# One more step of a weight conversion in five items of an attention head, and half the zero products in its last items

## The chip, the cores and the metric

The kernel runs on one core of one Trainium2 chip. The metric is the device time of one execution in microseconds (us). Its engines are named as in the profile: PE (TensorE, its weight loads as PEld), DVE (VectorE), ACT (ScalarE), POOL (GpSimd) and SP (SyncE, which here only issues DMAs).

## The reference, cut to what matters

```python
def reference(q, k, v, s, x..., w_in, w_out, domain_probs, w1, w2):
    # attention: 2 batches x 8 heads, 576 positions, 64 wide
    cum = np.cumsum(np.maximum(s, 0.0), axis=-1)
    bias = -(cum[:, :, :, None] - cum[:, :, None, :])
    scores = np.where(causal, -1e9, scale * q @ k.T + np.minimum(bias, 0.0))
    attn = softmax(scores)
    x = (attn @ v) with the heads side by side      # 1152 x 512
    # a layer of 512 -> 2048 -> 512
    h = x @ w_in
    x = np.maximum(0.01 * h, h) @ w_out
    # four experts of 512 -> 1024 -> 512
    p = domain_probs / (domain_probs.sum(-1, keepdims=True) + 1e-09)
    out += p[:, e:e + 1] * (np.maximum(x @ w1[e], 0.0) @ w2[e])     # for e in 0 to 3
```

All of it is fp32 in the reference. The kernel receives `w_in` and `w_out` as 64-bit numbers and turns them into the bits of fp32 values on the chip: that is the weight conversion that the change is about.

## The kernel before, in words

All work is in one function, `attention_moe_moe2`, and every instruction of an engine is recorded through one helper, so that all have the line L43 in the profile and are told apart by the names of their tiles. In the first phase, up to about 220 us, the order on each engine is the order in which the program is written (`fixed`), so an instruction waits for all that was written ahead of it on its engine. A product in fp32 quality is made from split operands: a value is cast to a rounded type (ACT, `CAST`) and the rest is what a subtraction leaves (DVE or POOL, `TENSOR_TENSOR`).

The first phase has three strands that are woven by hand.

- **Attention**, the generator `attention()` (`side`). It works in items; an item is one tile of 128 queries of one head. Its steps for an item are the scores (PE, `ps_sc`, then a custom instruction on DVE that adds the mask and takes the minimum, `z`), the exponential (ACT, `z<-z,mn`), the transposes (PE, `ps_pt`, copied by ACT to `pv`), the values (PE, `ps_o`) and, behind a pair of heads, the scaling (DVE `st`, `xo`) and the transposed result (PE `ps_x`, ACT and DVE `x`). Items overlap: while the scores of item i are made, the transposes are those of item i-3. The generator yields three times an item. The scores have two PSUM buffers, the transposes two, the values one.
- **The weight conversion**, the generator `supply()`. It has 16 units of 128 x 1024 numbers (512 KB of fp32). A unit's raw 64-bit numbers are fetched to a tile `r` (1024 KB, two buffers). Then come ACT `raw<-r` (absolute value and scale), two DVE `TENSOR_SCALAR` (limits, shift), two DVE `SCALAR_TENSOR_TENSOR raw<-r,raw` (bits, sign). A unit's finished fp32 numbers are stored to DRAM (`w_f<-raw`) and the unit after next is fetched. In the head of the phase (`heading`) the unit is also split on the spot, by an ACT `CAST w<-raw` of 128 x 1024 and a DVE `TENSOR_TENSOR w<-raw,w`, and store and fetch are issued on ACT's queue. Units converted behind the head store and fetch on POOL's queue, and their split is made by `late_splits()`: SP loads 512 KB back (`raw<-w_f`), and ACT and DVE split it in halves of 128 x 512. One call of `next(units_of_w)` makes one step: seven steps a unit in the head, six behind it.
- **The layer**, the generator `main`, whose products are `ps_u` and `ps_d` on PE, with `ht` on ACT and DVE.

The head is the loop `for at_ in range(3*64)` over attention's yields; it ends in item 39. In it `CONVERTING` lists the items below 31 whose third yield takes a step of the conversion; from item 31 on each takes one. At the first two yields of each item from 31 on, `onto_held()` lets PE multiply a tile of zeros (128 x 128, two records each: `ps_u<-idle`) onto a bank that is held for a sum; it changes no value. Behind the head the loop `for at_, i in enumerate(side)` weaves the three strands, and the loop over `main` behind it brings the rest of the layer, late splits and, on DVE and POOL, sums and products for the second half (`sums`, `t`, `w<-sums`).

Of the kernel before, what the change touches and what calls it, by code (L numbers as in the profile page):

```python
# [19 lines left out]
def attention_moe_moe2(ctx: ExitStack, tc: tile.TileContext, q, k, v, s, w_in, w_out, probs, w1, w2, out):  # L20
# [107 lines left out]
    def late_splits():  # L128

        nonlocal reading  # L130
        while len(ready) < CONVERTED:
            n = len(ready)
            if n < min(retired + WB + 2, stored):
                reading, raw = True, kept.pop(n, None)
                if raw is None:
                    raw = load_w(*stream[n][:3])
                    for _ in range(5):
                        yield
                while n >= retired + WB:
                    yield  # L140

                w = wpool.tile([P, 2, 1024], F32R, tag="w", name="w")
                for part in (slice(0, 512), slice(512, 1024)):
                    nc.scalar.copy(w[:, 0, part], raw[:, part])
                    (nc.gpsimd if n == CONVERTED - 1 else nc.vector).tensor_tensor(w[:, 1, part], raw[:, part], f32(w[:, 0, part]), ALU.subtract)
                ready.append(w.rearrange("p l (a b) -> p l a b", a=stream[n][1][0]))
                reading = False
            else:
                yield
# [564 lines left out]
    def idling(n):  # L714

        for _ in range(n):
            nc.tensor.matmul(nothing[:, :P], idle[:, :P], idle[:, :P], start=True, stop=True)
# [3 lines left out]
    def onto_held():  # L721

        nc.tensor.matmul(held[2][:, :P], idle[:, :P], idle[:, :P], start=False, stop=False, skip_group_check=True)
# [19 lines left out]
    def pads(pool):  # L743

        for i in range(3):
            x, y = (pool.tile([P, 2, half[0]], F32, name=f"{of}e{i}") for of in "qk")
            q_e.append(x)
            k_e.append(y)
        for i in range(3):
            nc.gpsimd.memset(k_e[i][D:], 0.0)  # L750
            nc.gpsimd.memset(q_e[i][D:], 0.0)
            nc.gpsimd.memset(q_e[i][D:DK], 1.0)
            if i == 0:
                nc.gpsimd.memset(mask, 0.0)
                nc.gpsimd.affine_select(mask[:, S - P :], mask[:, S - P :], [[-1, P]], ALU.is_ge, MASKED, 0, 1)
            for x in v_s[i : 4 if i == 2 else i + 1]:
                nc.gpsimd.memset(x[:, :, 0 :: 2 * D + 1], 1.0)
                nc.gpsimd.memset(x[: P - S % P, QT - 1], 0.0)
        ones = pool.tile([P, 2, QC], F32, name="ones")
        nc.gpsimd.memset(ones[D:DK], 1.0)  # L760
        for x in q_s:
            nc.gpsimd.memset(f32(x[:, :, 0, QC:]), 0.0)
        own = mask2[:, P - LAST :]
        nc.gpsimd.memset(mask2, 0.0)
        nc.gpsimd.affine_select(own, own, [[-1, LAST]], ALU.is_ge, MASKED, -D, 1)
        nc.gpsimd.memset(own[:D], 0.0)
        nc.gpsimd.affine_select(own[:D], own[:D], [[-1, LAST]], ALU.is_ge, MASKED, 0, 1)
        return ones
# [236 lines left out]
    def attention():  # L1005

        nonlocal ending
        items, starts, n = [], {}, 0
        i, split = 0, iter(())
        while n < units or i < len(items) + 8:  # L1010
            if n < units and i == len(items):
                u = Unit(n)
                starts[n] = i
                items += [(u, *of) for of in u.items]
                if n + 2 < units and not 0 <= n + 2 - 2 * NP < 2:
                    load_keys(n + 2)
                    if n + 2 < 2 * NP:
                        decay(n + 2, k_e[(n + 2) % 3])
                if n in (2 * NP - 3, 2 * NP - 2):
                    load_keys(n + 3)  # L1020
                n += 1
            if n < units - 1 and i == starts[n - 1] + 2:
                load_values(n + 1)
            if i == starts[n - 1] and 2 * NP <= n < units:
                split = split_keys(n)
            for step, lag in STEPS:
                if 0 <= i - lag < len(items):
                    u, *of = items[i - lag]
                    step(u, *of)
                if lag == 1:  # L1030
                    next(split, None)
                if lag == 0 and i in CAST_AT:
                    cast_keys(2 * NP + CAST_AT.index(i), lowest[0])
                if lag in (1, 3, 7):

                    late = i - 5 + (lag == 7)
                    ending = lag != 3 and 0 <= late < len(items) and items[late][1:] == items[late][0].items[-1]
                    yield i
            i += 1

    def hidden_pool(stack, n):
        nonlocal hpool
        hpool = stack.enter_context(tc.tile_pool(name="hpool", bufs=n))
# [6 lines left out]
    with ExitStack() as phase:  # L1050
        x_t[0] = phase.enter_context(tc.tile_pool(name="x0pool", bufs=1)).tile([P, 2, KD, sizes[0]], F32R, name="x0")
        wpool = phase.enter_context(tc.tile_pool(name="wpool", bufs=4))
        r64p = phase.enter_context(tc.tile_pool(name="r64p", bufs=2))

        OPENED = (24, 25, 26, 27, 28, 29, 31, 33, 35)

        CONVERTING = (*range(5, 16), *range(17, 31, 2))
        side, units_of_w, late, opened = attention(), supply(), late_splits(), 0
        nothing = ps_mm.tile([P, 512], F32, tag="mm", name="nothing")
        with tc.tile_pool(name="early", bufs=1) as early:  # L1060
            ones = pads(early)
            sums = cumulative()
            next(sums)
            main = mlps(phases[0])

            for at_ in range(3 * 64):
                i = next(side)
                if done == 2 * NP and at_ % 3 == 2:
                    break
                if at_ % 3 == 0 and i in (6, 8):  # L1070
                    nc.scalar.copy(q_s[i // 2 - 3][D:DK, 1, :, :QC], ones[D:DK])
                if at_ % 3 == 1:
                    if i < 18:
                        idling(2 if i < 6 else 1)
                    elif opened < len(OPENED) and i >= OPENED[opened] and opened < 3 * (done // 2):
                        next(main)
                        opened += 1
                if at_ % 3 < 2 and i >= 31:
                    onto_held()
                if at_ % 3 == 2:  # L1080
                    if i == 3:
                        fetch64(1)
                    if i in (3, 4, 5):
                        next(sums)
                    if i in CONVERTING or i >= 31:
                        next(units_of_w)
        hidden_pool(phase, 6)
        heading = False

        owed = 0  # L1090
        for at_, i in enumerate(side):
            if at_ % 3 < 2:
                owed += WOVEN * KD / (2.0 * (40 - 6))
                while owed >= 1.0:
                    next(main)
                    owed -= 1.0
            if at_ % 3 != 1:
                next(late, None)
            if (at_ % 3 != 1 or i % 3 == 0) and not ending:
                next(units_of_w, None)  # L1100
        attn.close()
        w7pool = ctx.enter_context(tc.tile_pool(name="w7pool", bufs=2, side="right"))
        sumpool = phase.enter_context(tc.tile_pool(name="sumpool", bufs=2))
        scratch = phase.enter_context(tc.tile_pool(name="scratch", bufs=2))
        t7pool = ctx.enter_context(tc.tile_pool(name="t7pool", bufs=1, side="right"))
        tokens = paired_steps(1, x_t[1], t7pool)
        banks.close()
        ps_mm = Eight(ps_mm, ctx.enter_context(tc.tile_pool(name="ps_more", bufs=5, space=PSUM)))

        sevens = first_sevens()  # L1110
        for m, _ in enumerate(main):
            if m % 2 == 0:
                next(late, None)
            if (m % 3 == 0 or m == 19) and m not in (12, 15):
                next(tokens, None)
            if m % 4 == 2:
                next(units_of_w, None)
            if m % 4 % 2 and m >= 4:
                next(sevens, None)
        for _ in sevens:  # L1120
            pass
        for _ in tokens:
            pass
# [72 lines left out]
```

## Time and profile before

| | us |
|---|---|
| median of three runs | 698.78 |
| the three runs | 698.61, 701.58, 698.78 |
| the profiled execution | 699.07 |
| its span, first to last instruction | 697.3 |
| busy in the span: PE, DVE, ACT, POOL | 677.7, 475.8, 352.5, 406.0 |

Times of rows are microseconds from the start of the span. A timeline row has the start, the busy time of the row's instructions, the engine, the line, the operation with its output and inputs, how many instructions are in the row, and in brackets how long the engine was idle ahead of it and what ended that. Starts of neighbouring instructions overlap a little, since an engine begins one before the other has left. The clock in the windows is the granted share of TensorE's full clock.

### The profile page before, as it was taken

Reading aid. Unit: us, or ns where it says so; the run is one execution under the profiler, and the core shown is the slowest. Engines: PE = TensorE matmul, PEld = TensorE weight load, DVE = VectorE, ACT = ScalarE, POOL = GpSimd, SP = SyncE. Lnnn points to the kernel's source line nnn. Section 1 sums busy time; section 2 is a strip of 40 time slices with the busy share of each in tenths; the row PEclk is TensorE's granted clock in tenths of the full one; section 3 lists DMA queues with packets and bytes.
Section 4 is the critical chain, followed back from the end, with each engine's and each line's share of the span. In section 5 each row is a group of like instructions: output and inputs, shape, how many; then the busy total and the mean of one; then the engine's idle time right before and its main releaser. Section 6 shows DMA issues by size and latency. Waiting matters only on the chain.

```text
span 697.3 us, 12008 instructions
## 1 busy us (share of the span) xinstructions
PE 677.7 (97%) x4496; PEld 623.7 (89%) x4496; DVE 475.8 (68%) x1040; ACT 352.5 (51%) x727; POOL 406.0 (58%) x386
## 2 busy tenths in 40 slices
PE   8899999899998999999999999999999999999998
PEld 7778778778787999999999989999899899998997
DVE  6878899998697458837855747647657376465564
ACT  5768978876544566533634525325244253261520
POOL 5100212221198887861997949949679498495830
PEclk9999999999999999999999999999999999999999
DMA  7798689746631321101011110111202111112003
GB/s 217 197 244 205 198 224 276 218 154 211 241 122 62 121 91 62 62 1 61 1 61 62 61 61 30 63 31 61 61 1 62 61 34 58 32 62 61 1 16 120
DMA packets 43050, 69.15 MB, mean 99 GB/s; under 512 B 6432, under 2 KB 26672, under 8 KB 42992
## 3 DMA queue, kind: packets, MB, share of 16 engines
q1 hardware_dynamic: 33744, 40.30, 19.9%
q0 software_dynamic: 6016, 20.71, 9.6%
q10 hardware_dynamic: 3232, 7.38, 3.3%
q8 instruction: 35, 0.57, 0.4%
q14 instruction: 23, 0.19, 0.1%
HBM read 57.54 MB, written 10.82 MB: 98 GB/s over the span
## 4 chain that ended last, share of the span: by engine, by line
PE 71%; DVE 8%; issue 8%; DMA 7%; ACT 3%; POOL 2%; SPq 0%; ACTq 0%; POOLq 0%; DVEq 0%
PE ps_d L43 35%; PE ps_u L43 33%; DMA r<-in_moe_w_out_dram 3%; DVE t L43 2%; DMA qr<-in_q_dram 2%; DMA r<-in_moe_w_in_dram 1%; PE ps_sc L43 1%; DVE sums L43 1%; DVE raw L43 1%; PE ps_o L43 1%; DVE z L43 1%; PE ps_pt L43 1%; DMA ke<-cum 1%; ACT raw L43 1%; DVE y L43 1%
## 5 line engine op out<-in xcount | busy, mean ns | idle before, releaser
L43 PE MATMUL ps_u<-t,w 128*128 128x320 f32 (+1 forms) x1680 | 237.7, 301 | 4.1 <-DVE t L43 2.9
L43 POOL TENSOR_TENSOR w<-raw,w 128x512 fp32r<-128x512 f32 (+2 forms) x118 | 185.9, 1595 | 94.2 <-ACT w L43 93.9
L43 PEld LDWEIGHTS ps_u<-t,w 128*128 128x128 f32 x1680 | 231.4, 191 | 5.5 <-DVE t L43 3.2
L43 PE MATMUL ps_d<-w,ht 128*128 128x256 f32 (+1 forms) x1164 | 195.4, 326 | 0.1
L43 PEld LDWEIGHTS ps_d<-w,ht 128*128 128x128 f32 x1164 | 173.3, 190 | 18.6 <-PE ps_u L43 0.4
L43 ACT CAST w<-raw 128x512 fp32r<-128x512 f32 (+2 forms) x138 | 98.2, 740 | 127.0 <-PE ps_d L43 69.7
L43 ACT ACTIVATE ht<-ps_u 128x320 fp32r<-128x320 f32 (+2 forms) x160 | 68.6, 439 | 99.2 <-DVE ps_u L43 71.1
L43 PE MATMUL ps_d<-ht,w 128*128 128x320 f32 (+1 forms) x576 | 109.1, 340 | 0.2 <-DVE ht L43 0.2
L43 PEld LDWEIGHTS ps_d<-ht,w 128*128 128x128 f32 x576 | 91.4, 188 | 6.6 <-DVE ht L43 0.6
L43 POOL TENSOR_TENSOR raw<-raw 128x256 f32<-128x256 f32 x120 | 86.2, 741 | 1.9
L43 DVE SCALAR_TENSOR_TENSOR oacc<-ps_d,pn,oacc 128x256 f32<-128x256 f32 (+1 forms) x92 | 51.5, 578 | 44.9 <-PE ps_d L43 44.2
L43 DVE TENSOR_TENSOR ps_u<-ps_u,tmp 128x320 f32<-128x320 f32 (+1 forms) x120 | 55.8, 469 | 31.5 <-PE ps_u L43 29.9
L43 DVE SCALAR_TENSOR_TENSOR ht<-ps_u,ht 128x320 fp32r<-128x320 f32 (+1 forms) x112 | 49.8, 455 | 16.8 <-ACT ht L43 16.5
L43 DVE TENSOR_TENSOR tmp<-ps_u,tmp 128x320 f32<-128x320 f32 (+1 forms) x80 | 36.9, 462 | 32.0 <-PE ps_u L43 24.5
L43 POOL DMA_DIRECT2D w_f<-raw x13 | 8.3, 637 | 85.3 <-DVE raw L43 71.8
L43 PE MATMUL ps_u<-x,w 128*128 128x512 f32 x192 | 55.7, 410 | 0.9 <-DVE x L43 0.9
L43 ACT ACTIVATE z<-z,mn 128x256 f32<-128x256 f32 (+4 forms) x72 | 42.5, 590 | 8.7 <-DVE mn L43 7.8
L43 DVE TENSOR_TENSOR ht<-ps_u,ht 128x320 fp32r<-128x320 f32 (+1 forms) x48 | 26.5, 553 | 26.8 <-ACT ps_u L43 26.6
L43 DVE CUSTOM_DVE_ANT_0 z<-ps_sc,mask 128x256 f32<-128x256 f32 (+4 forms) x72 | 35.9, 499 | 10.1 <-PE ps_sc L43 6.6
L43 POOL TENSOR_TENSOR ht<-sums,ht 128x1024 fp32r<-128x1024 f32 x16 | 38.6, 2409 | 6.3 <-ACT ht L43 6.3
L43 ACT COPY pv<-ps_pt 128x512 f32<-128x512 f32 (+3 forms) x80 | 33.2, 424 | 15.8 <-PE ps_pt L43 15.7
L43 PE MATMUL ps_pt<-ident,z 128*128 128x128 f32 x200 | 34.6, 276 | 5.9 <-ACT pv L43 4.9
(97 smaller groups left out, 773.5 us busy)
## 6 DMA issues: line engine op xcount, KB each, us to landing
raw<-in_moe_w_dram SPq DMA_DIRECT2D x32, 512.0 KB
raw<-w_f SPq DMA_DIRECT2D x21, 512.0 KB
w_f<-raw POOLq DMA_DIRECT2D x13, 512.0 KB, 3.5
r<-in_moe_w_out_dram POOLq DMA_DIRECT2D x6, 1024.0 KB, 8.6
r<-in_moe_w_in_dram POOLq DMA_DIRECT2D x5, 1024.0 KB, 8.4
r<-in_moe_w_in_dram ACTq DMA_DIRECT2D x3, 1024.0 KB
kd<-in_k_dram POOLq DMA_DIRECT2D x8, 288.0 KB, 7.6
kr<-in_k_dram SPq DMA_DIRECT2D x8, 288.0 KB
```

The lines of the kernel that those rows point to most:

```text
L43: ins = call(*args, **kw)
```

## The change

Two lines differ. `CONVERTING` gets the items 18, 20, 22, 24 and 26, so that each item from 17 to 27 takes a step. And from item 36 on `onto_held()` is called at an item's first yield alone.

```diff
-        CONVERTING = (*range(5, 16), *range(17, 31, 2))
+        CONVERTING = (*range(5, 16), *range(17, 28), 29)
...
-                if at_ % 3 < 2 and i >= 31:
+                if at_ % 3 < (2 if i < 36 else 1) and i >= 31:
                     onto_held()
```

The list before has items 17, 19, 21, 23, 25, 27, 29; the head therefore takes five steps more than before and goes five steps further in the conversion. Counted over the whole program: PE has 14 zero products in place of 18 and no other row that differs; one store of a converted unit and one fetch go from POOL's queue to ACT's; 512 KB are loaded back by SP for five weight tiles more, which are split in two halves of 128 x 512 in place of one piece of 128 x 1024. From the sums for the second half on (about 194 us) the order of every engine is as before.

ACT in the head, from about 30.5 us on, before (`x_108` is the transposed attention, `pv_102` and `pv_103` the transposed weights of attention, `raw<-r_363` the first step of the conversion's second unit counted from item 17; names with numbers are buffers):

```order
L43 CAST x_108<-ps_x 128x256
L43 ACTIVATE z<-z,mn 128x128
L43 COPY pv_102<-ps_pt 128x256
L43 ACTIVATE raw<-r_363 128x1024
L43 ACTIVATE z<-z,mn 128x128
L43 COPY pv_102<-ps_pt 128x256
L43 ACTIVATE z<-z,mn 128x256
L43 COPY pv_103<-ps_pt 128x128
L43 DMA w_f_76<-raw 128x1024
L43 DMA r_543<-in_moe_w_out_dram 128x2x1024
L43 CAST w<-raw 128x1024
L43 ACTIVATE z<-z,mn 128x256
```

and in the change:

```order
L43 CAST x_108<-ps_x 128x256
L43 ACTIVATE raw<-r_363 128x1024
L43 ACTIVATE z<-z,mn 128x128
L43 COPY pv_102<-ps_pt 128x256
L43 DMA w_f_76<-raw 128x1024
L43 DMA r_505<-in_moe_w_out_dram 128x2x1024
L43 CAST w<-raw 128x1024
L43 ACTIVATE z<-z,mn 128x128
L43 COPY pv_102<-ps_pt 128x256
L43 ACTIVATE z<-z,mn 128x256
```

The step `raw<-r_363` stands one exponential and one copy earlier, and the cast of the unit before it follows after one item in place of two.

DVE in the same place, from about 32.6 us on, before (`ISA` is the custom instruction of the scores and its read-out):

```order
L43 TENSOR_TENSOR xo<-ps_o,st 128x256
L43 ISA z,mn<-ps_sc,mask 128x256
L43 ISA mn 128x1
L43 ISA z,mn<-ps_sc,mask 128x128
L43 ISA mn 128x1
L43 ISA z,mn<-ps_sc,mask 128x128
L43 ISA mn 128x1
L43 TENSOR_TENSOR x_108<-ps_x,x_108 128x256
L43 TENSOR_TENSOR w<-raw,w 128x1024
L43 ISA z,mn<-ps_sc,mask 128x256
```

and in the change:

```order
L43 TENSOR_TENSOR xo<-ps_o,st 128x256
L43 TENSOR_TENSOR w<-raw,w 128x1024
L43 ISA z,mn<-ps_sc,mask 128x256
L43 ISA mn 128x1
L43 TENSOR_SCALAR raw<-raw 128x1024
L43 ISA z,mn<-ps_sc,mask 128x128
L43 ISA mn 128x1
L43 TENSOR_SCALAR raw<-raw 128x1024
L43 ISA z,mn<-ps_sc,mask 128x128
L43 ISA mn 128x1
L43 TENSOR_TENSOR x_108<-ps_x,x_108 128x256
L43 SCALAR_TENSOR_TENSOR raw<-r_363,raw 128x1024
```

The subtraction `w<-raw,w` now stands ahead of three more score instructions, and a step of the next unit stands between each two items.

ACT at the end of attention, from about 178 us on, before (`raw<-r_2136` is the first step of the last unit):

```order
L43 COPY pv_102<-ps_pt 128x4x128
L43 CAST w<-raw 128x512 x2
L43 COPY pv_103<-ps_pt 128x384
L43 ACTIVATE ht<-ps_u 128x512
L43 ACTIVATE ps_u<-ps_u 128x512
L43 COPY pv_103<-ps_pt 128x384
L43 ACTIVATE raw<-r_2136 128x1024
L43 ACTIVATE ht<-ps_u 128x512
```

and in the change, where it is `raw<-r_2061`:

```order
L43 COPY pv_102<-ps_pt 128x4x128
L43 CAST w<-raw 128x512 x2
L43 ACTIVATE raw<-r_2061 128x1024
L43 COPY pv_103<-ps_pt 128x384
L43 ACTIVATE ht<-ps_u 128x512
L43 ACTIVATE ps_u<-ps_u 128x512
L43 COPY pv_103<-ps_pt 128x384
L43 ACTIVATE ht<-ps_u 128x512
```

The last unit's first step has moved ahead of two copies and one pair of the layer.

## Rows read from the trace of the kernel before

**Rows 1.** The page: busy time of the engines in the span.
```profile
PE 677.7 (97%) x4496; PEld 623.7 (89%) x4496; DVE 475.8 (68%) x1040; ACT 352.5 (51%) x727; POOL 406.0 (58%) x386
```

**Rows 2.** Windows: stretch, length, busy time of PE to POOL, clock, DMA share, GB/s.
```profile
31.00:47.00 16.00, 14.87 (x100) 12.80 (x100) 10.92 (x39) 12.05 (x32) 0.78 (x2) 1.00 1.02 251
...
60.00:66.40 6.40, 6.40 (x47) 5.82 (x46) 5.49 (x15) 4.95 (x11) 0.58 (x1) 1.00 1.02 181
66.40:190.00 123.60, 119.55 (x775) 96.12 (x774) 108.29 (x216) 94.81 (x195) 26.88 (x44) 1.00 0.71 212
...
217.90:221.40 3.50, 3.50 (x15) 3.50 (x15) 1.14 (x3) 0.71 (x2) 3.50 (x4) 0.51 0.00 0
```

**Rows 3.** Waits of PE, 66.4 to 222 us: total us, times, longest us.
```profile
PE ps_pt L43 <- ACT pv L43: 3.7, 4, 1.7
PE ps_u L43 <- DVE t L43: 2.9, 1, 2.9
```

**Rows 4.** Timeline of ACT in the head.
```profile
31.91 1.13 ACT L43 ACTIVATE raw<-r 128x1024 f32<-128x1024 f32 x1 [0.49 <-DMA r<-in_moe_w_in_dram]
...
32.95 0.39 ACT L43 ACTIVATE z<-z,mn 128x128 f32<-128x128 f32 x1
...
34.05 1.05 ACT L43 CAST w<-raw 128x1024 fp32r<-128x1024 f32 x1
```

**Rows 5.** Timeline of DVE in the head.
```profile
32.97 0.41 DVE L43 CUSTOM_DVE_ANT_0 z<-ps_sc,mask 128x256 f32<-128x256 f32 x1
...
36.30 1.21 DVE L43 TENSOR_TENSOR w<-raw,w 128x1024 fp32r<-128x1024 f32 x1
...
43.10 0.42 DVE L43 CUSTOM_DVE_ANT_0 z<-ps_sc,mask 128x256 f32<-128x256 f32 x1 [0.22 <-PE ps_sc L43]
```

**Rows 6.** Timeline of PE in the head.
```profile
34.62 0.39 PE L43 MATMUL ps_sc<-ke,qe 128*128 128x128 f32 x2
...
45.27 0.55 PE L43 MATMUL ps_o<-vs,pv 128*128 128x65 f32 x4
...
48.93 0.50 PE L43 MATMUL ps_u<-x,w 128*128 128x512 f32 x1 [0.91 <-DVE x L43]
...
58.38 0.30 PE L43 MATMUL ps_pt<-ident,z 128*128 128x128 f32 x1 [0.75 <-DVE x L43]
```

**Rows 7.** Timeline of PE: one zero product and the row behind it.
```profile
46.89 0.39 PE L43 MATMUL ps_u<-idle 128*128 128x128 f32 x2
47.11 0.38 PE L43 MATMUL ps_pt<-ident,z 128*128 128x128 f32 x2
```

**Rows 8.** Timelines of ACT and of PE just behind the head.
```profile
70.34 1.12 ACT L43 ACTIVATE raw<-r 128x1024 f32<-128x1024 f32 x1
71.37 0.74 ACT L43 COPY pv<-ps_pt 128x512 f32<-128x512 f32 x2
...
71.99 0.66 PE L43 MATMUL ps_pt<-ident,z 128*128 128x128 f32 x4 [0.40 <-ACT pv L43]
```

**Rows 9.** Waits of ACT, 66.4 to 190 us, then its timeline at the longest.
```profile
ACT raw L43 <- DMA r<-in_moe_w_out_dram: 10.3, 4, 5.5
...
183.61 1.14 ACT L43 ACTIVATE raw<-r 128x1024 f32<-128x1024 f32 x1 [5.51 <-DMA r<-in_moe_w_out_dram]
```

**Rows 10.** The tile r: duration ns min/median/max of one form, and time of its fetches.
```profile
L43 DVE SCALAR_TENSOR_TENSOR raw<-r,raw x32: 1184/1218/1226, 17.6 to 191.6; 128x1024 uint32<-128x1024 uint32 x32
...
DMA to landing us min/median/max: 6.2/8.4/10.2
```

**Rows 11.** Timelines of POOL and of DVE at the start of the second half's sums.
```profile
193.07 0.55 POOL L43 DMA_DIRECT2D w_f<-raw  x1 [11.32 <-DVE raw L43]
...
202.78 0.69 DVE L43 TENSOR_TENSOR ht<-ps_u,ht 128x512 fp32r<-128x512 f32 x1 [0.97 <-ACT ps_u L43]
...
213.93 3.05 DVE L43 TENSOR_TENSOR t<-sums,t 128x1280 fp32r<-128x1280 f32 x1
```

**Rows 12.** The tile t: duration ns min/median/max of one form on DVE.
```profile
L43 DVE TENSOR_TENSOR t<-sums,t x6: 1358/1488/3049, 203.9 to 331.4; 128x1280 fp32r<-128x1280 f32 x4, 128x1024 fp32r<-128x1024 f32 x2
```

## The prediction

> **What bounds the kernel now.** I read the page's busy times first: PE works for 97% of the span [rows 1], so an edit gains only where it shortens PE's own list or one of its waits, and loses only where it makes a new one. Then the windows by stage, since the change lies between about 30 and 194 us. From 31 to 47 us nothing is full: PE is busy for 14.87 of 16.00 us, DVE for 10.92, ACT for 12.05 [rows 2]. PE runs in short pieces there and each hands over to DVE (score) or ACT (exponential, copy). From 60 to 66.4 us PE is busy all the time [rows 2]; this is where the zero products stand. From 66.4 to 190 us PE is busy for 119.55 of 123.60 us and DVE for 108.29 [rows 2], so DVE is the engine that can least take more work. Last I read the waits: between 66.4 and 222 us PE waits 3.7 us in four places for ACT's copy `pv`, and once 2.9 us for DVE's `t` [rows 3]. The bound to keep in mind: everything that the middle could give back is about 4 us.
>
> **The change, part by part.** The sum is made on the profiled execution, 699.07 us, which is 0.29 above the median of the runs shown, 698.78.
>
> *Steps in items 18 to 26.* The head does the same steps in the same order, but earlier. Between items 17 and 27 there were six steps and now there are eleven. Those that come in are, on DVE, two `SCALAR_TENSOR_TENSOR` of 1.22 us [rows 10] and one `w<-raw,w` of 1.21 [rows 5], and on ACT one `raw<-r` of 1.13 and one `CAST` of 1.05 [rows 4]. That is 3.6 us more for DVE and 2.2 for ACT in a stretch in which DVE has 16.00 - 10.92 = 5.1 us free and ACT 3.95. Bounds: 0, if all of it falls into gaps, and 3.6, if all of DVE's share ends on PE. Where it falls I get by walking the new order through the timeline. The first `raw<-r` stands earlier in the program, but it already waited for its transfer until 31.91 [rows 4], so it starts no earlier; instead the exponential and the copy that ran ahead of it now wait behind it. The cast that follows then ends near 34.65, and `w<-raw,w` stands ahead of the score instruction that ran at 32.97 [rows 5]. With 1.21 us for the subtraction and 0.41 for the score that one ends near 36.2. PE's scores of 34.62 [rows 6] need the buffer it empties and move to about 36.3, 1.7 us late. The second `raw<-r` now comes in item 25, near 39 us. Its fetch is issued behind the first store, about 33 us as before, and takes 6.2 to 10.2 us, 8.4 in the median [rows 10], so it lands near 41.5: ACT stands for about 2 us, and what is queued behind it there is exponentials and copies, for which PE waits. The cast and the subtraction of this unit follow in items 26 and 27 and push the score of 43.10 [rows 5] to about 46.2, and the values of 45.27 [rows 6] to about 47.9: 2.6 us late. Behind 47 us the steps are as many as before, three of them are shorter, and PE had waits of its own, 0.91 at 48.93 and 0.75 at 58.38 [rows 6], which partly swallow the lateness: I carry 2.4 us to the end of the head. **Term: +2.4, bounds 0 and +3.6.**
>
> *Four zero products fewer.* One costs PE the distance to the row behind it, 47.11 - 46.89 = 0.22 us [rows 7]; four are 0.88. They go at the second yield of items 36 to 39, just ahead of transposes that wait for ACT or DVE. There the third unit's cast and subtraction have just been added, so I let most of it turn into waiting. **Term: -0.1, bounds -0.9 and 0.**
>
> *Just behind the head.* The fourth `raw<-r`, 1.12 us on ACT at 70.34, stood right ahead of the copy for which PE waited 0.40 at 71.99 [rows 8]. It is now in item 34. **Term: -0.4, bounds -0.4 and 0.**
>
> *The middle.* Five more weight tiles are split from copies loaded back by SP, with the same number of elements on ACT and DVE; the instructions are halves. One store and fetch pair leaves POOL's queue, which is busy for 26.88 of 123.60 us here [rows 2], and costs nothing. What changes is where the remaining `raw<-r` stand against their transfers. ACT waited 10.3 us for these in four places, the longest 5.5 at 183.61 [rows 9]; from that long one PE lost nothing, because its waits in this stretch sum to 3.7 us for `pv` and the longest is 1.7 [rows 3]. Each of these steps now stands elsewhere, and at the places of the two longest waits of PE stand casts. Between getting back all 3.7 and a new wait like the longest, 1.7, I take a gain of 1.0, since DVE is nearly full and gives the rest back. **Term: -1.0, bounds -3.7 and +1.7.**
>
> *The second half's start.* The order is as before there. The product behind the wait of 2.9 [rows 3] needs `t`, which DVE makes at 213.93 in 3.05 us [rows 11]; DVE had been held until 202.78 by PE's own products [rows 11], so it moves with PE. **Term: 0, bounds -3.3 (the second rival) and 0.**
>
> Sum: 2.4 - 0.1 - 0.4 - 1.0 = +0.9, so 699.97 on the profiled execution and **699.7** for the median. By the terms' nearer bounds this case runs from 697.5 to 701.7. A measurement here tells about 0.5% from no change, 3.5 us: below 695.3 is faster, above 702.3 slower.
>
> **The rivals.**
>
> *The second and third fetch come late (slower).* If the fetch for the step in item 25 takes 10.2 us [rows 10] it lands at 43.3, and ACT stands for nearly 4 us with everything of attention behind it, 1.8 more than in my walk; the next one, in item 34, would be later by the same on a chain that has no slack left, another 1.7. That gives 699.7 + 3.5 = 703.2. For it: the DMA engines are full from 31 to 47 us (share 1.02 [rows 2]). Against: the median is 8.4. It decides when a fetch takes over some 9.5 us. Chance 0.14.
>
> *POOL starts the second half's work earlier (faster).* POOL's last store at 193.07 had waited 11.32 us for DVE's `raw` [rows 11], which goes back to ACT's 5.5 us at 183.61 [rows 9]. The last unit's first step now stands earlier. If POOL is ahead by a few us, it has finished when DVE makes the last `t`, and that takes 1.49, the median of its kind, instead of 3.05 [rows 12]: 1.56 less on PE's wait. A wait that is 1.4 long may also leave the clock alone, which stood at 0.51 for 3.50 us behind the wait of 2.9 [rows 2]: 1.7 more. 699.7 - 3.3 = 696.4. Against it: POOL's products behind the store also wait for weights from SP and for PE. The Trainium skill ("SBUF — State Buffer", section "Who interferes with whom") says that a DVE instruction with two SBUF inputs contends with a GpSimd instruction that reads SBUF; the 3.05 beside 1.49 agrees, and by that rule it is the overlap alone that decides. Chance 0.12.
>
> *The head hides all of it (faster).* DVE's 5.1 free us [rows 2] take the 3.6: +2.4 becomes 0, and the zero products give 0.8 more. 699.7 - 3.2 = 696.5. Against it is the place: the subtraction stands directly ahead of a score. Chance 0.13.
>
> *The clock falls with fewer zeros.* A stretch at 0.51 as long as the one seen, 3.50 us [rows 2], costs 1.7: 701.4. Against it: the clock is 1.00 from 31 to 47 us [rows 2], where PE runs transposes and small products and no zeros at all. The Trainium skill ("TensorE: Matmul & The Clock Gate", section "Part 4: PE-mode transpose") says that transposes do not count as busy in the way that products do, which speaks against dropping products beside them; the 1.00 of that stretch does not bear it out as a danger here. Chance 0.04.
>
> That the change does nothing is excluded by the order: the zeros and the steps do move.
>
> **How the numbers follow.** 0.57 for the forecast, 0.14, 0.12, 0.13 and 0.04 for the rivals. Slower by over 0.5% is most of the first rival, 0.11, and a tail of the forecast, 0.02: 0.13. Faster by over 0.5% needs both gains together, or one with more from the middle: 0.08. The rest, 0.79, is the same. The range leaves out about 0.12 above 702.5 and 0.08 below 695.8.
>
> **What would show it.** Right: `w<-raw,w` ahead of a score near 34.7 and PE's scores behind it some 1.7 us late; an ACT wait for `r` of about 2 us near 39 to 41; PE's first `ps_u<-x` near 51 in place of 48.93; the products of zeros gone and waits for DVE in their place; the `pv` waits of the middle at 1 to 3 us in sum; the wait for `t` at 2.9 again. Wrong: PE's rows of 47 us on time (the head hides it), an ACT wait over 3.5 us in the head (the first rival), the last `t` at 1.5 us (the second), or a clock of 0.5 between 60 and 70 us.

## The result, and the profile after

The changed kernel takes 704.36 us in the median of six runs (703.65 to 706.00), beside 698.76 of the kernel before in six (698.61 to 701.58): the ratio is 1.008, with a 95% interval of 1.0056 to 1.0103. It is **slower by 0.8%**, about 5.6 us. The forecast of 699.7 was wrong, and 704.36 lies above the range (695.8 to 702.5). The profiled execution after took 706.00 us with a span of 704.2, 6.9 more than the one before (699.07). One execution of all, the one profiled in e11_lead_5 below, ran at a granted clock of 0.56 throughout and took 1099.65 us; the ratio of e11 leaves it out.

The page after, busy time of the engines in the span (columns as in [rows 1]):

```profile
PE 680.8 (97%) x4488; PEld 625.2 (89%) x4488; DVE 473.1 (67%) x1045; ACT 353.2 (50%) x732; POOL 403.8 (57%) x384
```

The engines are hardly busier than before (PE's 3.1 us more go with a lower clock). Where the time went is seen by setting PE's rows beside the same rows of before. Timeline of PE after, at the places where its lateness grows or shrinks:

```profile
34.95 0.49 PE L43 MATMUL ps_sc<-ke,qe 128*128 128x128 f32 x2
...
43.15 0.44 PE L43 MATMUL ps_pt<-ident,z 128*128 128x128 f32 x2 [1.42 <-ACT pv L43]
...
48.36 0.33 PE L43 MATMUL ps_pt<-ident,z 128*128 128x128 f32 x1 [1.84 <-ACT pv L43]
...
64.30 0.41 PE L43 MATMUL ps_pt<-ident,z 128*128 128x128 f32 x1 [2.00 <-DVE x L43]
...
78.99 0.60 PE L43 MATMUL ps_pt<-ident,z 128*128 128x128 f32 x4
...
111.50 0.33 PE L43 MATMUL ps_pt<-ident,z 128*128 128x128 f32 x1 [2.21 <-ACT pv L43]
...
225.48 2.76 PE L43 MATMUL ps_u<-t,w 128*128 128x320 f32 x17 [1.86 <-DVE t L43]
```

The same rows before, where [rows 6] does not have them (the row of 111.50 is the last of the five of 102.11, which started at 102.54):

```profile
41.33 0.38 PE L43 MATMUL ps_pt<-ident,z 128*128 128x128 f32 x2
...
44.46 0.27 PE L43 MATMUL ps_pt<-ident,z 128*128 128x128 f32 x1
...
102.11 0.71 PE L43 MATMUL ps_pt<-ident,z 128*128 128x128 f32 x5
...
217.04 9.86 PE L43 MATMUL ps_u<-t,w 128*128 128x320 f32 x55 [2.92 <-DVE t L43]
```

PE is late by 0.3, 1.8, 3.9, 5.9, 7.0 (78.99 beside 71.99 [rows 8]), 9.0 and 8.4 us. Ahead of its wait for `t` it is 9.5 late (225.48 - 1.86 beside 217.04 - 2.92). Between 217 and 221 of before it wins back another 1.5, and 7.0 stays. So some 7 us are lost in the head and 2.5 in the middle, whose one large new wait is near 110 us; and 2.5 come back at the end of the phase.

Timeline of ACT after, in the head:

```profile
30.64 1.15 ACT L43 ACTIVATE raw<-r 128x1024 f32<-128x1024 f32 x1
...
41.43 1.12 ACT L43 ACTIVATE raw<-r 128x1024 f32<-128x1024 f32 x1 [2.35 <-DMA r<-in_moe_w_out_dram]
...
43.00 0.38 ACT L43 CAST x<-ps_x 128x256 fp32r<-128x256 f32 x1
45.83 0.34 ACTq L43 DMA_DIRECT2D w_f<-raw  x1
46.21 0.45 ACTq L43 DMA_DIRECT2D r<-in_moe_w_out_dram  x1
46.70 1.04 ACT L43 CAST w<-raw 128x1024 fp32r<-128x1024 f32 x1 [3.33 <-DMA qr<-in_q_dram]
```

ACT is stopped twice. The first stop, 2.35 us in item 25, waits for the fetch of `r`. The second is at the issue of a store: ACT finishes a cast at 43.4, the store `w_f<-raw` of item 26 is issued at 45.83, and the cast behind it runs at 46.70, 3.33 us late. The profile names a load of `qr` as what ended it. The program's list of waits says why the two are tied (ACT's fetch of item 19, SP's load, ACT's store):

```
L43 DMA r64_505<-in_moe_w_out_dram 128x2x1024 [waits DMAHW5_49]
L43 DMA qr_579<-in_q_dram 64x2x256 [waits DMAHW5_49]
L43 DMA w_f32_76<-raw_487 128x1024 [waits DMAHW5_49]
```

In this program the transfers that SP and ACT issue take eight completion semaphores in turn, and an issue waits until the transfer that had the same one has landed. So SP's load of `qr` stood until the fetch had landed (41.41; issued at 41.42; before, the first of these at 38.26), and ACT's store stood until that load had landed (45.81; issued at 45.83).

Windows after (columns as in [rows 2]); the eighth column is the granted clock:

```profile
47.00:50.00 3.00, 1.03 (x4) 0.55 (x4) 2.15 (x6) 3.00 (x8) 0.00 (x0) 1.00 1.12 325
50.00:53.00 3.00, 2.81 (x16) 2.84 (x17) 2.72 (x8) 2.09 (x6) 0.00 (x0) 0.61 1.03 382
53.00:56.00 3.00, 3.00 (x18) 2.83 (x17) 2.08 (x5) 1.75 (x5) 0.00 (x0) 0.82 0.44 118
63.00:66.00 3.00, 1.70 (x5) 1.45 (x6) 1.88 (x5) 1.71 (x5) 0.00 (x0) 0.72 0.40 123
66.00:70.00 4.00, 4.00 (x26) 3.95 (x26) 1.95 (x6) 2.91 (x7) 0.58 (x1) 0.78 1.01 290
110.00:115.00 5.00, 3.50 (x12) 2.93 (x13) 4.84 (x11) 4.08 (x11) 1.10 (x2) 0.71 0.79 237
214.00:230.00 16.00, 14.14 (x78) 12.51 (x77) 14.36 (x18) 6.37 (x11) 15.78 (x11) 1.00 0.09 33
```

PE is busy for 1.03 of 3.00 us from 47 to 50, and behind that the clock drops to its lower level for part of the time: 0.61, then 0.82. It does so again behind the 2.00 us wait at 64.30 and behind the 2.21 at 111.50. Length times what is missing to 1.00 gives 1.2 + 0.5 + 0.8 + 0.9 + 1.5 = 4.9 us, 3.4 of them in the head. Before there was one such stretch, 3.50 us at 0.51 [rows 2], 1.7 us. So, by this estimate, up to 3.2 of the 6.9 us between the two executions are clock; it is an upper one, since PE is not busy all the time in these windows. At the end of the phase it is the other way round: the clock stays at 1.00 in this execution.

### The profile page after: what moved, and what is told of

Same layout as the page of the kernel before. It is cut to its first block, busy times and chain, and to the rows that moved or that the text cites. A ratio compares the mean times of both kernels' runs of the same rounds, so it can differ in the third digit from the quotient of the medians.

```text
span 704.2 us, 12012 instructions
## 1 busy us (share of the span) xinstructions
PE 680.8 (97%) x4488; PEld 625.2 (89%) x4488; DVE 473.1 (67%) x1045; ACT 353.2 (50%) x732; POOL 403.8 (57%) x384
## 4 chain that ended last, share of the span: by engine, by line
PE 72%; DVE 11%; DMA 8%; issue 3%; ACT 3%; POOL 1%; ACTq 0%; DVEq 0%; POOLq 0%
PE ps_d L43 35%; PE ps_u L43 33%; DVE raw L43 3%; DMA r<-in_moe_w_out_dram 2%; DMA raw<-w_f 2%; DVE z L43 2%; DVE t L43 2%; PE ps_o L43 1%; DMA r<-in_moe_w_in_dram 1%; DVE sums L43 1%; PE ps_pt L43 1%; PE ps_sc L43 1%; DVE w L43 1%; DVE ht L43 1%; DVE y L43 1%
## 5 line engine op out<-in xcount | busy, mean ns | idle before, releaser
L43 POOL DMA_DIRECT2D w_f<-raw x12 | 6.8, 565 | 72.3 <-DVE raw L43 59.7
L43 PEld LDWEIGHTS ps_pt<-ident,z 128*128 128x128 f32 x200 | 25.3, 144 | 20.4 <-ACT pv L43 12.3
```

Source lines behind the costliest of these rows:

```text
L43: ins = call(*args, **kw)
```

## The experiments

Theory at first: ACT's two stops make the loss, and the clock falls because PE starves behind them. Rivals: the engine time of the added steps (3.6 us on DVE, 2.2 on ACT); the four missing zero products. Ratios are against the kernel before, run on the same chip, with 95% intervals.

| run | ratio | interval |
|---|---|---|
| the change | 1.0080 | 1.0056 to 1.0103 |
| e1_steps_only | 1.0125 | 1.0093 to 1.0157 |
| e2_zeros_only | 0.9994 | 0.9974 to 1.0015 |
| e3_later_third | 1.0090 | 1.0056 to 1.0124 |
| e4_pool_queue | 1.0095 | 1.0059 to 1.0132 |
| e5_late_send | 1.0045 | 1.0019 to 1.0071 |
| e6_late_both | 1.0025 | 1.0003 to 1.0048 |
| e7_more_traffic | 1.0102 | 1.0063 to 1.0142 |
| e8_first_on_pool | 1.0091 | 1.0063 to 1.0119 |
| e9_traffic_later | 1.0021 | 1.0004 to 1.0037 |
| e10_lead_3 | 0.9973 | 0.9952 to 0.9993 |
| e11_lead_5 | 1.0024 | 1.0005 to 1.0042 |
| e12_store_early | 1.0061 | 1.0024 to 1.0098 |

### One line of the change at a time

e1_steps_only, to the changed kernel:

```diff
-                if at_ % 3 < (2 if i < 36 else 1) and i >= 31:
+                if at_ % 3 < 2 and i >= 31:
```

> The change's items, with two zero products an item as before. If the loss comes from ACT being stopped twice in the head (2.35 us for a fetch in item 25, 3.33 us ahead of the cast in item 26), the zeros do little: 703 to 705, both stops there again, PE's first layer product behind 47 us still some 5 us late. If the loss comes from the four missing zeros (clock 0.72 between 63 and 66 us): 699 to 701.

e2_zeros_only, to the kernel before:

```diff
-                if at_ % 3 < 2 and i >= 31:
+                if at_ % 3 < (2 if i < 36 else 1) and i >= 31:
```

> The items of before, with one zero product an item from item 36 on. If ACT's stops are the cause: 698 to 699, clock 1.00 up to 75 us. If the missing zeros are the cause: 701 to 705, with a granted clock under 1.00 between 60 and 75 us.

The steps alone take 707.47 us, more than was expected, the zeros alone 698.75. Four zero products fewer change nothing that can be measured in the kernel before. Putting them back into the change doesn't mend it: the median is higher than the change's, with intervals that still touch, and the clock falls all the same. Windows in e1:

```profile
50.00:53.00 3.00, 3.00 (x15) 3.00 (x16) 2.55 (x7) 1.68 (x6) 0.00 (x0) 0.50 1.03 361
53.00:56.00 3.00, 3.00 (x14) 2.71 (x13) 2.08 (x5) 1.93 (x5) 0.00 (x0) 0.50 0.28 68
66.00:70.00 4.00, 4.00 (x20) 3.94 (x19) 0.80 (x5) 2.65 (x5) 0.58 (x1) 0.57 0.81 262
```

The missing zeros are out as a cause. The loss is in the list of items.

### Taking ACT's stops away

e3_later_third moves the third unit's first step from item 25 to 27, and the store, the fetch and the cast that follow it from 26 to 28:

```diff
-        CONVERTING = (*range(5, 16), *range(17, 28), 29)
+        CONVERTING = (*range(5, 16), *range(17, 25), *range(27, 31))
```

> Items 17 to 24 and 27 to 30 carry a step: as many steps up to item 31 as in the change, but the third unit's first step, the store and the cast stand two items later, when the fetch has had time. If ACT's stops are the cause: both are under 0.5 us, 699 to 700.5. If it is the engine time of the added steps (3.6 us on DVE, 2.2 on ACT), it is spent all the same: 702.5 to 704.5.

e4_pool_queue issues the store and the fetch of item 26 on POOL's queue:

```diff
-            queue = nc.scalar if heading else nc.gpsimd
+            queue = nc.scalar if heading and n != 2 else nc.gpsimd
```

> The change, with the store and the fetch of item 26 issued on POOL's queue in place of ACT's. If the issue of that store is what held ACT for 3.33 us ahead of the cast: the stop goes, the first one of 2.35 us stays, the clock of 50 to 53 us rises from 0.61 to over 0.9, 700 to 702. If something else held the cast: 703.5 to 705 and the stop of 3.3 us is still there.

Neither came out as the theory says: 704.49 and 705.76 us. The number of e3 even lies where the rival, engine time, had put it. The stops shrank: in e3 the one for `r` is gone and the one at the store is 1.54 us, in e4 the one for `r` is 1.01 and the one at the store is gone. But another wait stood in their place. Timeline of PE in e4:

```profile
56.11 0.71 PE L43 MATMUL ps_sc<-kd,qs 66*128 66x448 f32 x1 [3.93 <-DMA kd<-cum_d]
```

PE itself now waits for an input of attention, 3.93 us here, 1.9 in e3. So the stops of ACT cannot be the whole cause. What the change, e3 and e4 have in common is that the second fetch of 1 MB is issued at 43 to 46 us, in the midst of SP's loads of `qr`, `kr`, `vs` and `kd`. Before, it was issued at 53.3. That made a new theory: the fetch falls among attention's own loads and makes them late, whoever then waits for them. In the change itself that was ACT, at the issue of its store; PE's waits of over 1 us in the head are those for `pv` and `x` shown above, none for a load.

### Putting the store and the fetch back

e5_late_send keeps the steps up to item 33 and issues the store and the fetch of item 26 in item 33. It takes no step in items 34 to 39, so the head's lead of five steps is gone, and it has two zero products an item:

```diff
-        def send(n, raw):
+        def send(n, raw, now=False):
             nonlocal sent
+            if heading and n == 2 and not now:
+                delayed.append((send, n, raw))
+                return
...
-                if at_ % 3 < (2 if i < 36 else 1) and i >= 31:
+                if at_ % 3 < 2 and i >= 31:
...
+                    if i == 33:
+                        send, n, raw = delayed.pop()
+                        send(n, raw, True)
-                    if i in CONVERTING or i >= 31:
+                    if i in CONVERTING or 31 <= i <= 33:
```

> The change's steps in items 17 to 33, but the store and the 1 MB fetch of item 26 are issued in item 33, where the kernel before has them; no step in items 34 to 39, so the head ends with as many steps as before, and two zero products an item. New theory: the loss comes from that fetch, which now falls into attention's own loads (qr, kr, vs, kd from 41 to 50 us) and makes them late, whoever then waits for them. Then only the stop of some 2.3 us for the fetch in item 25 is left: 699.5 to 702. If it is the engine time of the steps in items 18 to 27, it is all there still: 703 to 705.

e6_late_both is the same with the items of e3:

> As the run with the late store and fetch, and the third unit's first step in item 27 in place of 25 (items 17 to 24 and 27 to 30 carry a step). If the early fetch is the cause: no stop of ACT over 0.5 us, no wait of PE for kd, 698 to 700.5. If it is engine time: 702.5 to 704.5.

Both came out as the new theory says, 700.58 and 699.79 us, though e5's stop for `r` is longer than expected. Waits of ACT between 31 and 60 us (columns as in [rows 3]), first e5:

```profile
ACT raw L43 <- DMA r<-in_moe_w_out_dram: 4.2, 1, 4.2
ACT z L43 <- DVE mn L43: 2.4, 3, 1.1
```

then e6:

```profile
ACT z L43 <- DVE mn L43: 4.5, 5, 1.6
...
ACT raw L43 <- DMA r<-in_moe_w_in_dram: 0.7, 1, 0.7
```

e6 has the steps of items 18 to 24 early, thus their engine time, but neither of the two stops and no early transfer. PE's row of 58.38 [rows 6] is 0.8 late there, in place of 5.9. Timeline of PE in e6:

```profile
59.17 0.33 PE L43 MATMUL ps_pt<-ident,z 128*128 128x128 f32 x1 [1.56 <-ACT pv L43]
```

What is left is 0.25% (0.03 to 0.48), 0.2 to 3.3 us. That bounds the engine time of the steps, which my prediction took for the main cost, from above; it does not exclude the 2.4 us of the forecast. The clean pair is e3 and e6, which have the same items up to 30 and differ in when the store and the fetch go out: 1.0090 and 1.0025, intervals apart. They differ in four zero products, too, which e2 prices at nothing, and in the lead behind the head: five steps of lead, put into the middle, cost 0.24% in e11 below, so that not all of the 0.65% need be the transfers. e5 differs from e6 by the stop for `r` in item 25; the two intervals overlap, so what that stop costs is not settled.

### The transfer without the steps

e7_more_traffic leaves every step of the kernel before in its place and adds a copy of 1 MB from DRAM to DRAM in item 26, issued at 39.64 us; e9_traffic_later adds the same copy behind the head, at 83.90. The edit of e7:

```diff
+    spare = dram.tile([P, 2, 1024], U32, name="spare")
...
+                    if i == 26:
+                        nc.gpsimd.tensor_copy(released, lowest[0])
+                        nc.gpsimd.dma_start(spare, stream[4][0])
```

> The kernel before, with one more transfer of 1 MB from DRAM to DRAM, issued on POOL's queue in item 26 behind that item's minimum; no step moves. If traffic in attention's loads is the cause: waits for qr, vs or kd of 1.5 to 4 us on ACT or PE between 47 and 57 us that the kernel before does not have, and 700.5 to 705. If engine time or ACT's order is the cause: 698 to 699.5.

> The kernel before with the same extra transfer of 1 MB from DRAM to DRAM as the run with more traffic, but behind the head (about 72 us), where the profile before shows DMA shares near 0.5. If the place of the transfer, among attention's loads, makes the loss: 698 to 700, not over 0.3% above before. If 1 MB more costs this much anywhere: 701 to 704.

With the copy in item 26 the kernel takes 703.45 us, 1.02% more, and the trace shows the same picture as e4 though no step of the conversion moved. Timeline of PE and windows in e7:

```profile
50.48 0.71 PE L43 MATMUL ps_sc<-kd,qs 66*128 66x448 f32 x1 [1.69 <-DMA kd<-cum_d]
```
```profile
47.00:53.00 6.00, 3.67 (x15) 3.25 (x16) 3.44 (x8) 1.13 (x2) 0.00 (x0) 0.76 0.95 179
53.00:60.00 7.00, 7.00 (x41) 6.49 (x40) 3.92 (x12) 5.88 (x13) 0.00 (x0) 0.72 0.70 219
```

PE is busy for 3.67 of 6.00 us, and the clock in the two windows is 0.76 and 0.72, which is 1.4 + 2.0 = 3.4 us (an upper estimate as above). The same megabyte behind the head costs 0.21% (0.04 to 0.37), and from 47 to 60 us the clock of e9 is 1.00. So it is the place of the transfer, among attention's loads, that costs; the copy also writes 1 MB, so its price is not exactly that of a fetch.

### The tie by the semaphore, and the store alone

e8_first_on_pool takes the fetch of item 19 off the semaphore that SP's load waits for:

```diff
-                fetch64(len(r64s), queue)
+                fetch64(len(r64s), nc.gpsimd if heading and n == 1 else queue)
```

> The change, with the fetch of item 19 alone on POOL's queue (its store stays on ACT's). In the change SP's next load of qr waits from 38 to 41.4 us until that fetch has landed, since both use the same completion semaphore; on POOL's queue it uses another. If this hold of SP is a main part of the loss: SP's qr loads are issued near 38 us, the stop of ACT ahead of the cast in item 26 falls under 1 us, 700 to 702. If it is the amount of traffic at that time, whoever issues it: 703 to 706, with the waits at another place.

It takes 704.78 us, as the change does. SP now issues the first two of its four `qr` loads at 36.38 and 37.47, but the stop ahead of the cast shrinks only from 3.33 to 2.93. Waits in the timeline of ACT in e8:

```profile
40.42 1.12 ACT L43 ACTIVATE raw<-r 128x1024 f32<-128x1024 f32 x1 [2.17 <-DMA r<-in_moe_w_out_dram]
...
45.30 1.04 ACT L43 CAST w<-raw 128x1024 fp32r<-128x1024 f32 x1 [2.93 <-DMA qr<-in_q_dram]
```

That SP is held until the fetch lands is thus not the main part; the loads themselves come late: the store now shares its semaphore with the load of 36.38, which lands at 44.41. This run shows something else too: of its five executions one took 699.89 us with a mean clock of 1.000, the other four 703.42 to 706.18 with 0.995 to 0.990. Both stops are in the first one, which is the one profiled. The kernel before took 695.98 and 696.55 us in its two executions at 1.000 on the same chip. So without any drop of the clock 3.3 to 3.9 us of loss remain, about half of it; the other half is paid when the clock drops. That rests on a single execution of e8.

e12_store_early is made from the change and has the store of 0.5 MB in item 26, the fetch alone in item 33, and, as e5, two zero products an item and no step behind item 33:

```diff
-            if len(r64s) < CONVERTED:
+            if len(r64s) < CONVERTED and not (heading and n == 2):
...
+                    if i == 33:
+                        fetch64(len(r64s))
-                    if i in CONVERTING or i >= 31:
+                    if i in CONVERTING or 31 <= i <= 33:
```

> As the run with the late store and fetch, but the store of 0.5 MB stays on ACT's queue in item 26; the 1 MB fetch alone moves to item 33. If ACT's stop at the issue of that store (3.3 us, until a load of qr with the same completion semaphore has landed) is the main part of the loss: the stop is there again, the clock falls behind it, 702.5 to 705. If the fetch among attention's loads is the main part: 699.5 to 701.5, as the run with both late.

The median is 703.78 us, in the range that was put down for the store as the main part. But the ratio, 1.0061, has a wide interval: it lies between e5 and the change and is not to be told from either, nor from e6. Timeline of ACT in e12:

```profile
43.77 1.12 ACT L43 ACTIVATE raw<-r 128x1024 f32<-128x1024 f32 x1 [3.71 <-DMA r<-in_moe_w_out_dram]
46.59 0.36 ACTq L43 DMA_DIRECT2D w_f<-raw  x1
46.99 1.04 ACT L43 CAST w<-raw 128x1024 fp32r<-128x1024 f32 x1 [1.28 <-DMA qr<-in_q_dram]
```

The stop at the store is there, 1.28 us. How the loss is shared between the store's issue and the fetch behind it stays open; that the two together, early in the head, carry most of it is what e3 and e6 show, with e7 for the transfer alone.

### The gain at the end, without the head

Near 217 us the changed kernel wins back 2.5 us, 1.0 by a shorter wait and 1.5 by the clock. Last `t` on DVE and POOL's product ahead of it, after:

```profile
223.95 1.48 DVE L43 TENSOR_TENSOR t<-sums,t 128x1280 fp32r<-128x1280 f32 x1
```
```profile
220.04 3.04 POOL L43 TENSOR_TENSOR w<-sums,w 128x1024 fp32r<-128x1024 f32 x1
```

POOL's product before:

```profile
212.97 2.67 POOL L43 TENSOR_TENSOR w<-sums,w 128x1024 fp32r<-128x1024 f32 x1
```

After, POOL's product ends at 223.08, ahead of DVE's `t`, which takes 1.48 us; before, it ran from 212.97 to 215.64 and `t`, begun at 213.93, took 3.05 [rows 11]. e10_lead_3 looks for that alone, with the head of the kernel before:

```diff
-            if (at_ % 3 != 1 or i % 3 == 0) and not ending:
+            if (at_ % 3 != 1 or i % 3 == 0 or i in (70, 74, 76)) and not ending:
```

> The head of the kernel before, and three more steps of the conversion in items 70, 74 and 76, behind the head. In the change the wait of PE for t ended earlier (1.9 us in place of 2.9) and the clock stayed at 1.00 behind it, 2.7 us in sum. If that came from the last unit standing earlier: 695 to 697.5, the wait for t under 2.2 us. If it was chance of that execution: within 0.3% of before.

It takes 696.87 us, ratio 0.9973 (0.9952 to 0.9993): **faster than both kernels**, if by little. DVE, PE and windows in e10:

```profile
214.37 1.48 DVE L43 TENSOR_TENSOR t<-sums,t 128x1280 fp32r<-128x1280 f32 x1
```
```profile
215.90 2.31 PE L43 MATMUL ps_u<-t,w 128*128 128x320 f32 x14 [1.88 <-DVE t L43]
```
```profile
214.00:217.00 3.00, 1.12 (x8) 1.10 (x8) 2.91 (x4) 0.00 (x0) 3.00 (x3) 1.00 0.01 3
217.00:221.00 4.00, 4.00 (x30) 4.00 (x29) 2.49 (x6) 2.01 (x6) 3.20 (x3) 1.00 0.13 43
```

PE's wait is 1.88 us in place of 2.9 [rows 3], and the clock behind it stays at 1.00 in place of 0.51 [rows 2]. So an earlier last unit is enough to shorten the wait.

Two things limit this. e7, with every step where the kernel before has it, has a wait of 1.88 us for `t` as well; PE is 3.4 us late there (220.47 beside 217.04), and nothing else is seen that could put POOL ahead. In the change both hold, the lead and a lateness, and no run tells them apart. And the clock's part is not certain: e1, e3 and e4 wait for `t` for 1.88 us too, and behind it their clock is 0.50 (227 to 230 us), 0.57 (225 to 229) and 0.57 (226 to 230). Timeline of DVE and of PE in e7, then the window of e1:

```profile
218.93 1.48 DVE L43 TENSOR_TENSOR t<-sums,t 128x1280 fp32r<-128x1280 f32 x1
```
```profile
220.47 3.86 PE L43 MATMUL ps_u<-t,w 128*128 128x320 f32 x14 [1.88 <-DVE t L43]
```
```profile
227.00:230.00 3.00, 3.00 (x13) 3.00 (x12) 1.17 (x3) 0.00 (x0) 3.00 (x3) 0.50 0.00 0
```

e11_lead_5 puts five more steps in items 44, 46, 50, 52 and 56:

> The head of the kernel before, and five more steps in items 44, 46, 50, 52 and 56, behind the head: the lead that the change has, without its transfers in attention's loads. If the loss of the change is that of the head alone, and its gain at the end real: 695 to 698. If the lead costs DVE's time in the middle as well: 699 to 702.

It takes 701.02 us, 0.24% more (0.05 to 0.42): a miss for the gain, and in the range put down for a lead that costs in the middle. So a lead as long as the change's is not free there; where in the middle it costs stays open.

## Why the prediction was wrong, point by point

**The step that failed** is the term "Steps in items 18 to 26", +2.4 with bounds 0 and +3.6. It counted the engine time of the moved steps and the wait for `r`, and walked them through the timeline, but it left out two instructions that stand between the steps: the store and the fetch that item 26 issues on ACT's queue. The pair was on ACT's queue before, too, at 52.92 and 53.31 us in item 33; with the step it moved to 45.83 and 46.21. The store's issue stopped ACT for 3.33 us, and the 1 MB behind it went among attention's loads. The head lost about 7 us instead of 2.4: up to 3.4 by the clock, the rest, some 3.6, by waits. The order that stands ahead of the prediction shows such a pair right ahead of the first cast, but the only pair that the text priced is another one, further back: "One store and fetch pair leaves POOL's queue ... and costs nothing". It did not ask what moves on ACT's.

**The clock was not in the term.** The prediction had it as a rival about missing zeros (0.04). It did fall, by up to 3.2 us more than before, and the sign that the prediction named for this rival, a low clock between 60 and 70 us, was there (0.72 and 0.78). But e1, with all the zeros, has it too (0.57 from 66 to 70 us); e1 and e2 exclude the zeros, and on that point the rival's reason was rightly doubted (the stretch from 31 to 47 us that it was doubted by is not quite without zeros: one stands at its end, 46.89 [rows 7]). In the change the clock fell each time behind a wait of PE. That such a wait always brings it down is not so: in e5 PE waited 3.25 us and the clock stayed at 1.00, in this stretch and in the whole execution. Timeline and window of e5:

```profile
44.45 0.44 PE L43 MATMUL ps_pt<-ident,z 128*128 128x128 f32 x2 [3.25 <-ACT pv L43]
```
```profile
41.00:47.00 6.00, 2.75 (x17) 2.20 (x17) 2.07 (x5) 4.27 (x10) 0.00 (x0) 1.00 0.56 133
```

Within the term, the walk was right on one thing and right by chance on another. The first `w<-raw,w` ran at 33.32, not near 34.7, since `r` had landed earlier this time and `raw<-r` started at 30.64; PE's scores were 0.3 late there, not 1.7. The second `raw<-r` ended its wait at 41.43, as forecast ("near 41.5"), but the fetch was issued at 31.28 and took 10 us, not 8.4. In e5 it took 12.

**Zero products** (-0.1): right within what can be told, e2 gives 0.9994 (0.9974 to 1.0015).

**Just behind the head** (-0.4): right; at the row of 71.99 [rows 8] PE's lateness shrinks by 0.5.

**The middle** (-1.0): wrong in sign. Of PE's waits at the two longest places one shrank from 1.70 to 0.73 us and the other, 1.00, went, as forecast. But a cast of a tile that SP loads back came late (below), PE waited 2.21 us behind it at 111.50, and the clock stood at 0.71 from 110 to 115. Timeline of ACT after:

```profile
105.81 1.14 ACT L43 CAST w<-raw 128x512 fp32r<-128x512 f32 x2 [3.02 <-DMA raw<-w_f]
106.85 1.16 ACT L43 ACTIVATE raw<-r 128x1024 f32<-128x1024 f32 x1
107.92 0.46 ACT L43 COPY pv<-ps_pt 128x384 f32<-128x384 f32 x1
```

The five tiles more that are loaded back were priced at nothing, because their elements are the same; their transfers are not. From the head's end to its wait for `t` PE lost 2.5 us more, up to 1.5 of it by this clock, where I had a gain of 1.0. That the loads cause it is read from this one trace; no run has them without the early steps.

**The second half's start** (0): the second rival happened, 2.5 us of its 3.3. That a `t` clear of POOL's product shortens PE's wait is shown by e10; that it was the earlier last unit which put POOL ahead in the change is not, since e7 has the same without it. The Trainium skill ("SBUF — State Buffer", section "Who interferes with whom") says that a DVE instruction with two SBUF inputs contends with a GpSimd instruction that reads SBUF, that the port pair they share is an exclusive lock, and that issue order decides who blocks. The rows agree: 3.05 us where POOL's product, from 212.97 to 215.64, had started ahead of `t`, 1.48 where it had ended ahead of it. So it is not the overlap alone that decides, as the prediction has it: after, POOL's next instruction starts at 223.98, 0.03 us behind `t`, and runs beside it, and `t` takes 1.48.

**The first rival** (703.2, chance 0.14) gave nearly the measured time, but not by its mechanism: the fetch did take over 9.5 us, which was its condition, but it had been issued earlier, so that `r` landed at 41.4 and not at 43.3. It was the stop at the store, and with it attention's loads, that I had no case for.

## What to carry to other kernels

A step that is moved takes its transfers along: ask of each of them what is on the DMA queues at the new place, who loads at that time, and what the issue itself waits for on the engine that issues it. Here the engines showed free time and the DMA share was at 1.02 [rows 2], and it was the transfers that decided whether a step could go there. And allow, behind a new wait of PE, for what the clock may then cost, which in the head here was, by the estimate above, about as much as the waits themselves.

## What the runs showed that was not expected

An issue of a store on ACT's queue stopped ACT for 1.28 us (e12), 2.93 (e8) and 3.33 (the change), because the completion semaphore it takes in turn belonged to a transfer of another engine that had not landed; the profile showed it only as idle time of the cast behind it. One kernel with two such stops (e8) took 699.89 us with a mean clock of 1.000 and 703.42 to 706.18 with 0.995 to 0.990, so its times spread with the clock. And the same 1 MB cost 1.02% in item 26 and 0.21% behind the head.
